# Skip term of tiles 12 to 14 on VectorE, one column of ones for four heads, gate copies and turn-matrix casts on either engine, and a new work list

## The chip, the cores and the metric

One Trainium2 chip; the kernel runs on one of its NeuronCores. A core has TensorE (PE: matmuls, and PEld for its weight loads, which overlap them), VectorE (DVE), ScalarE (ACT), GpSimd (POOL), SyncE (SP, which here only issues transfers) and 16 DMA engines. Each engine runs its instructions in order. Matmuls write to PSUM, eight banks of 512 fp32 columns here; VectorE and ScalarE move results from there to SBUF, which frees the bank. The metric is device microseconds of one execution, the median of several runs.

## The reference, cut to what matters

For x of 2048 rows and 512 columns, a state-space layer and a linear attention with softmax features, mixed by a gate:

```python
g = sigmoid((x * gate_w).sum(-1, keepdims=True))
a = 2 * real(C @ h) + x * Dskip              # h: scan over rows, h = Lam_bar*h + B_bar x
q, k, v = x @ wqkv                           # 32 heads of 16
phi(t) = concat(softmax(t @ w_phi), softmax(-t @ w_phi))
kv = phi(k)^T v ;  z = sum over rows of phi(k)
b = (phi(q) @ kv) / (phi(q) @ z + 1e-6) @ wo
out = g * a + (1 - g) * b
```

## The kernel before

The 2048 rows are 16 tiles of 128. Everything is issued by a list of tokens, `ORDER` (lines 24 to 54), which is walked once: each token resumes a generator that issues the instructions of one small step, so the list sets the order on every engine. A token may carry `@b` (the PSUM bank that the step takes) and `:D` (the step's copy runs on VectorE; without it on ScalarE, through `evac`, line 139, or `scaled`, line 468).

The tokens that matter here:

- `Lk`, `Lx`, `Lv`, `Lb`, `Lq`, `Lc`, `Lo`, `Ld`: loads on SP's queue. `Lx` gives two plain loads of x (tiles 0 and 1) and then seven transposing loads into `xT`, two tiles each (tiles 2 and 3 by the first, 10 and 11 by the fifth; line 244). `Lv` loads the v weights into `WKV` (267), `Lb` the two halves of B into `C2` (249) and transposes them into `BT` (252). `Ld` loads the skip vector, and the rows of x for the tiles in `XD`, into space that `WKV` no longer needs.
- `Z`: small matmuls on zeros that keep TensorE at work at the start. `W`, `T`, `f`: transposes of the k weights and of x's first tiles, and the folding of the feature weights into the k weights.
- `k0` to `k15`: key features of a tile, four matmuls of 480 columns (521), then a cast into `Xq`. `v0` to `v15`: values of a tile, four matmuls of 512 columns (521), then a cast into one of eight buffers `vx`. `q0` to `q15`: query features, 481 columns, of which the last is the gate's logit; after the cast a step writes the clamped, negated logit into `nge` (555).
- `x`, `n`, `e`, `s` with a group of key tiles (`X`, `N`, `E`, `S` of query tiles): maximum, minimum, exponentials and sums of the softmax features. `a`: the sums over keys, 128x128 weights against 68 columns of `vx` (645): four heads of 16 values, and a column of ones behind each head. `Y`: these sums through a mask into `KVm` (845, 847).
- `b`, `g`, `z`, `sa`, `sb`, `H`: the scan over rows: matmuls with `BT` (655, 660), with the turn matrices `dg` (672 to 690, 757 to 773), and additions into `HH` (750). `Da`, `Db`: the turn matrices, three casts into `dgv` each (458, 460) and products (463) on VectorE.
- `hd`, `hk`, `ek`, `dk`: scaled copies (470, 472) and additions that make the remaining rows' states `LS`.
- `y0` to `y15`: the state-space output of a tile: eight 512-column matmuls (876) and, for a tile outside `XD`, the skip term as four 128-column matmuls (883). `o`: attention numerators (893), a reciprocal by way of logarithm and exponential, and a product on VectorE (907). `O`: their transposes by DMA. `t`: four matmuls with `wo` (932) and the scaling by the gate `G` (938 on ScalarE, 940 on VectorE). `u`: for a tile in `XD` the gated skip term on VectorE (912), added in the tile's evacuation (936). `G`: the gate from `nge`. `R`: the stores.

Tile numbers of `y`, `o`, `t` follow the order of the output, not of `x`. `y0` and `o0` come after the sums over keys are complete.

Of the kernel before, what the change touches and what calls it, by code (L numbers as in the profile page):

```python
# [14 lines left out]
BF16 = mybir.dt.bfloat16  # L15
# [10 lines left out]
f1 f0 T0:D Lx f2@4 V@3 T1@2 f3@6 Lx V f2 Z k0@5 P T1:D U P f3 k1@2 k1 Lv P2 P k0 P2 U k3@1 P2 k2@6 P2 k7@4 P2 P4 P3  # L26
P2 P3 P4 U Lx P4 i i M i Lb x0z U k5@0 k4@3 k1 M k3 k0 V2@1 i k7 i v0@4 n0 k5 x0 M k2 Lb v1@6 x0 n0 V2 k6@2 Lx v6@1
k4 i v3@3 k8@5 n0 x0 n0 x1 k9@0 n1 x0 Lx x1 L x0 n1 k10@7 n0 k6 v1 x2 M2 M2 Lx Lb x2 v6 e0 k11@2 x1 n1 x2 Lb k8 n1
x1 x2 x1 Da k13@5 v3 v0 Lq n2 k12@4 k15@3 k14@1 n1 dc n2 e1 s0 k9 k11 n2 x2 n2 b10@0 Da k15 k14 n2 Lc k10 s0 b10 k13
# [20 lines left out]
S3 y11 dk0 S3 dk2:D t8 dk0:D dk0 dk0 dk2 R3 dk0 t9 dk2 O5 dk0 dk4 dk2 t10 dk4:D dk4 dk2 dk4:D y14@6 t8 dk4 t10 t11  # L50
t9 S3 dk6:D o12@4 o13@1 S3 dk6 o12 R4 y13@3 y12@7 o12 dk6:D o13 dk4 o13 o12 o14@4 o13 dk6 o14 R2 o14 dk6 dk6 y15@12
o14 y13 y12 o15@4 u11 y12 o15 y14 t11 o15 y14 y13 O6 t12 O7 R5 t13 t14 o15 O8 t12:D t13:D t14:D y15 R6 R7 y15 t15
t15 R8 t15 t15:D R8
# [27 lines left out]
def kernel(  # L81
# [57 lines left out]
    def evac(out_ap, in_ap):  # L139
        if sel["eng"] == "act":  # L140
            nc.scalar.copy(out=out_ap, in_=in_ap)  # L141
        else:
            nc.vector.tensor_copy(out=out_ap, in_=in_ap)
# [171 lines left out]
    m16 = maskN[:].rearrange("p a b -> p (a b)")  # L315
    order = [2 * g + q for g in ORD for q in range(2)]
    live = {}
    MM = nc.tensor.matmul
# [134 lines left out]
        yield  # L453

    def st_D(k0, k1):
        TT, TC = VT, nc.vector.tensor_copy
        nk = k1 - k0
        TC(out=dgv[0:HS, k0:k1].rearrange("p k m h f -> p k h m f"), in_=dgs[0:HS, k0:k1].unsqueeze(4).to_broadcast([HS, nk, 2, MT, 4]))
        for h in range(2):
            TC(out=dgv[HS:P, k0:k1, :, h, :], in_=dgs[HS:P, k0:k1, 1 - h].unsqueeze(3).to_broadcast([HS, nk, MT, 4]))  # L460
# [81 lines left out]
    def st_v(ti):  # L542
        pv = bank([P, D], F32, "pv")
        tile_mm(pv, KO[ti], Wv)
        yield
        evac(vxb[ti % NVX][:, :, 0:Dh], pv[:].rearrange("p (h e) -> p h e", e=Dh))
        yield

    def st_q(n):
# [4 lines left out]
        yield
        VS(out=nge[:, n:n + 1], in0=pq[:, DF:DF + 1], scalar1=-Z_MAX, scalar2=-1.0, op0=ALU.max, op1=ALU.mult)
# [93 lines left out]

# [369 lines left out]
```

## Time and profile before

| | us |
|---|---|
| median of 3 runs (146.64 to 147.11) | 146.94 |
| the profiled execution's own time | 146.7 |
| its span, first to last instruction of the profile | 144.7 |
| TensorE busy | 138.2 |
| VectorE busy | 132.9 |
| ScalarE busy | 125.4 |
| GpSimd busy | 21.9 |

In the rows below, times are microseconds from the span's start, a row of the chain or timeline gives start, duration and what ran, `x24` is a number of instructions merged into the row, `[0.18 <-DMA ...]` says that the engine stood idle that long before it and what ended the wait. In a row of a group, what follows the bar is total busy time, mean ns of one instruction, and idle time before them. A row of windows gives for each engine the busy time and number of instructions. Matmuls are pipelined and their ends are modelled, so that TensorE's busy time contains short waits; these are found from the starts of successive rows.

### The profile page before, as it was taken

To read this page: it belongs to the slowest core of one execution; us is meant where nothing else is said; L and a number is where in the kernel's file an instruction comes from. 1 tells how busy PE (TensorE), PEld (TensorE's weight loads), DVE (VectorE), ACT (ScalarE), POOL (GpSimd) and SP (SyncE) were. 2 spreads that over 40 slices of the span, in tenths; PEclk is the share of its full clock that TensorE was granted. 3 is DMA by queue.
4 is the path that set the end of the run, shared out by engine and by line. 5 is a ranking of instruction groups with operands and counts; after the bars stand their busy time and mean duration, and the time that the engine had idled before them with its cause. 6 is when DMAs were issued, how large, how long until landed. Compare 5 with 4: busy or idle time off the path is not lost.

```text
span 144.7 us, 2815 instructions
## 1 busy us (share of the span) xinstructions
PE 138.2 (96%) x971; PEld 74.9 (52%) x986; DVE 132.9 (92%) x313; ACT 125.4 (87%) x245; POOL 21.9 (15%) x40
## 2 busy tenths in 40 slices
PE   6999999999999999999999999999999999999990
PEld 4854444444545465544445556656454545455550
DVE  5389999999999999999999999999999999999560
ACT  0899998999999999999999999999999996984110
POOL 7100807900000000190000336000000000000000
PEclk9999999999999999999999999999999999999998
DMA  4999998997030058079929857886896989995441
GB/s 115 219 231 230 202 184 201 174 212 131 5 70 2 0 128 239 0 67 107 181 64 210 211 89 116 146 173 150 202 112 127 273 189 243 210 290 163 117 137 36
DMA packets 55957, 21.56 MB, mean 149 GB/s; under 512 B 44552, under 2 KB 55944, under 8 KB 55944
## 3 DMA queue, kind: packets, MB, share of 16 engines
q1 hardware_dynamic: 52688, 18.98, 63.1%
q0 software_dynamic: 2240, 2.10, 11.1%
q10 hardware_dynamic: 1016, 0.32, 0.9%
q8 instruction: 7, 0.11, 0.4%
q14 instruction: 6, 0.05, 0.1%
HBM read 3.30 MB, written 2.10 MB: 37 GB/s over the span
## 4 chain that ended last, share of the span: by engine, by line
PE 79%; DMA 9%; SPq 4%; DVE 3%; issue 1%; ACT 1%; ACTq 0%
PE PS L521 20%; PE PS L876 17%; PE PS L660 10%; PE PS L655 10%; PE PS L932 9%; DMA xT<-in_A_x_dram 7%; PE PS L645 3%; SPq L244 3%; PE PS L893 2%; DMA CS<-in_B_wqkv_dram 2%; PE PS L672 2%; PE PS L883 2%; DVE HH L750 1%; PE PS L678 1%; SPq L249 1%
## 5 line engine op out<-in xcount | busy, mean ns | idle before, releaser
L594 ACT ACTIVATE EE<-EE 128x2048 bf16<-128x2048 bf16 x16 | 31.8, 2002 | 0.5 <-DVE EE L587 0.5
L521 PE MATMUL PS<-WKV,xT 128*128 128x480 bf16 (+1 forms) x124 | 28.8, 373 | 0.4 <-DMA xT<-in_A_x_dram 0.2
L521 PEld LDWEIGHTS <-xT 128*128 128x128 bf16 x192 | 18.3, 99 | 19.1 <-DMA xT<-in_A_x_dram 0.6
L876 PE MATMUL PS<-C,LS 128*128 128x512 bf16 (+1 forms) x102 | 22.7, 362 | 0.1
L141 ACT CAST Xq<-PS 128x480 bf16<-128x480 f32 x32 | 19.0, 640 | 0.2
L655 PE MATMUL PS<-xT,BT 128*128 128x512 bf16 x64 | 16.1, 379 | 0.0
L141 ACT CAST LS<-PS 128x512 bf16<-128x512 f32 x24 | 15.8, 735 | 0.1
L521 PE MATMUL PS<-Wq,xT 128*128 128x481 bf16 x64 | 15.6, 368 | 0.0
L660 PE MATMUL PS<-xT,BT 128*128 128x512 bf16 x64 | 15.5, 379 | 0.0
L932 PE MATMUL PS<-Wo,oT 128*128 128x512 bf16 (+2 forms) x64 | 14.8, 366 | 0.2
L569 DVE TENSOR_TENSOR EE<-EE 128x256 bf16<-128x256 bf16 (+3 forms) x54 | 14.6, 302 | 0.0
L876 PEld LDWEIGHTS <-LS 128*128 128x128 bf16 x104 | 9.3, 98 | 9.3 <-DVE LS L822 0.3
L938 ACT ACTIVATE ot<-PS,G 128x512 bf16<-128x512 f32 (+1 forms) x11 | 7.0, 671 | 5.4 <-PE PS L932 5.3
L907 DVE TENSOR_TENSOR on<-PS,rd 128x512 bf16<-128x512 f32 x16 | 10.6, 680 | 0.5 <-ACT rd L901 0.4
L470 ACT ACTIVATE CT<-HH,dgs 128x512 bf16<-128x512 bf16 x16 | 11.1, 722 | 0.0
L569 DVE TENSOR_TENSOR EE<-Xq 128x1024 bf16<-128x1024 bf16 (+1 forms) x18 | 11.0, 623 | 0.0
L141 ACT CAST vx<-PS 128x512 bf16<-128x512 f32 x16 | 10.9, 710 | 0.0
L470 ACT ACTIVATE CT<-CS,nsn 128x512 bf16<-128x512 bf16 x15 | 10.6, 726 | 0.0
L580 DVE TENSOR_TENSOR EE<-Xq,EE 128x2048 bf16<-128x2048 bf16 (+1 forms) x9 | 10.0, 1110 | 0.0
L587 DVE TENSOR_TENSOR EE<-EE,Xq 128x2048 bf16<-128x2048 bf16 (+1 forms) x9 | 9.9, 1105 | 0.0
L660 PEld LDWEIGHTS <-BT 128*128 128x128 bf16 x64 | 6.1, 98 | 6.9 <-issue 0.2
L932 PEld LDWEIGHTS <-oT 128*128 128x128 bf16 x68 | 6.2, 98 | 6.6 <-DMA oT<-on 0.7
(175 smaller groups left out, 252.7 us busy)
## 6 DMA issues: line engine op xcount, KB each, us to landing
out_dram<-ot SPq DMA_DIRECT2D x7, 256.0 KB, 2.5
C<-CS SPq DMA_DIRECT2D x4, 256.0 KB, 3.1
C<-CT POOLq DMA_DIRECT2D x4, 256.0 KB, 8.3
CS<-HH SPq DMA_DIRECT2D x8, 128.0 KB, 3.4
LS<-CT POOLq DMA_DIRECT2D x4, 256.0 KB, 3.7
CS<-LS SPq DMA_DIRECT2D x2, 512.0 KB, 6.4
WKV<-in_B_wqkv_dram SPq DMA_DIRECT2D x1, 512.0 KB, 4.7
C<-in_A_B_re_dram SPq DMA_DIRECT2D x1, 512.0 KB, 6.4
```

Of the source, the lines that this page charges most:

```text
L141: nc.scalar.copy(out=out_ap, in_=in_ap)
L470: nc.scalar.mul(out=out_ap, in_=in_ap, mul=s_)
L521: MM(out=pt[:], lhsT=xT[:, kt, ti * P:(ti + 1) * P], rhs=W[:, kt, 0:pt.shape[-1]], start=(kt == 0), stop=(kt == KT - 1))
L569: VT(out=dst, in0=cur[:, :, :, 0:n, :], in1=cur[:, :, :, n:2 * n, :], op=op)
L580: VT(out=half(EE, 0), in0=X5, in1=live["mx", p].to_broadcast([P, L, 8, Dh, 4]), op=ALU.subtract)
L587: VT(out=t, in0=live["mn", p].to_broadcast([P, L, 8, Dh, 4]), in1=X5, op=ALU.subtract)
L594: aexp(out=EE[:, l_:l_ + w], in_=EE[:, l_:l_ + w], func=ACT.Exp)
L655: MM(out=pt[:], lhsT=BT[:, m, kt, :], rhs=cells(kt, r), start=(kt == 0), stop=False, skip_group_check=True)
L660: MM(out=pb[:], lhsT=BT[:, m, kt, :], rhs=cells(kt, 2 * pr), start=(kt == 0), stop=(kt == KT - 1))
L876: MM(out=py[:], lhsT=hs[m], rhs=C2[:, m, c:c + w], start=(m == 0), stop=False)
L907: VT(out=live["on", g_][:, u], in0=pn[:, :, :, 0:Dh], in1=rd[:].unsqueeze(3).to_broadcast([P, 2, 16, Dh]), op=ALU.mult)
L932: MM(out=py[:], lhsT=oT[:, g, :], rhs=Wo[:, g, c:c + w], start=False, stop=(g == HG - 1))
```

## The change

1. `XD`, the tiles whose skip term runs on VectorE, is now 12, 13 and 14, and not 10 and 11.
2. A `vx` buffer holds 65 columns for four heads, 64 values and one column of ones, and not 68; `a` multiplies by 65 columns, and `Y` takes the one sum for all four heads.
3. The step that writes a tile's gate logit into `nge` is a plain copy, on ScalarE unless the token has `:D`; clamp and negation are a first step of `G`, for eight tiles at once.
4. The casts of `Da` and `Db` go through `evac` too, so to ScalarE unless the token has `:D`.
5. `ORDER` is a new list.

```diff
-Lk Z@0 Lk Z Z Z Z B Z B Z Z Z Z Z Lx Lx Z Z Z Z W00@2 Lx W01@1 W00 W01 W00 W01 W10@3 W11@4 W11:D f1@2 f0@1 T0@5 W10
...
+B B Lk Z@0 Z Lk Z Z Z Z Z Z Z Z W01@1 Lx Z W00@2 Z W01 W00 Lx W01 Z Z W00 W11@3 W10@1 T0@2 f1@4 f1 f0@5 W11:D V@3 Lx
...
-XD = (10, 11)
+XD = (12, 13, 14)
...
+    AW = 4 * Dh + 1
...
-    vxb = [pAC.tile([P, H, Dh + 1], BF16, name=f"vx{k}") for k in range(NVX)]
+    vxb = [pAC.tile([P, NB, AW], BF16, name=f"vx{k}") for k in range(NVX)]
...
     def st_D(k0, k1):
-        TT, TC = VT, nc.vector.tensor_copy
+        TT, TC = VT, evac
...
-        evac(vxb[ti % NVX][:, :, 0:Dh], pv[:].rearrange("p (h e) -> p h e", e=Dh))
+        evac(vxb[ti % NVX][:, :, 0:AW - 1], pv[:].rearrange("p (m x) -> p m x", m=NB))
...
-        VS(out=nge[:, n:n + 1], in0=pq[:, DF:DF + 1], scalar1=-Z_MAX, scalar2=-1.0, op0=ALU.max, op1=ALU.mult)
+        evac(nge[:, n:n + 1], pq[:, DF:DF + 1])
...
-                   rhs=vxb[n_ % NVX][:, 4 * m:4 * m + 4, :].rearrange("p h e -> p (h e)"),
+                   rhs=vxb[n_ % NVX][:, m, :],
...
     def st_G(g):
         ns = slice(8 * g, 8 * g + 8)
+        VS(out=nge[:, ns], in0=nge[:, ns], scalar1=-Z_MAX, scalar2=-1.0, op0=ALU.max, op1=ALU.mult)
+        yield
```

What the new list does is seen in the instructions of an engine. First the start of SP's queue; `C_69` takes the two halves of B, `WKV` the v weights. Before:

```order
L235 DMA CS<-in_B_wqkv_dram 128x512 x2
L240 DMA CS<-in_A_x_dram 128x512 x2
L244 DMA_TRANSPOSE xT<-in_A_x_dram 128x4x256 x3
L267 DMA WKV<-in_B_wqkv_dram 128x4x512
L244 DMA_TRANSPOSE xT<-in_A_x_dram 128x4x256
L249 DMA C_69<-in_A_B_re_dram 64x8x512
L249 DMA C_69<-in_A_B_im_dram 64x8x512
L244 DMA_TRANSPOSE xT<-in_A_x_dram 128x4x256 x3
L252 DMA_TRANSPOSE BT<-C_69 128x8x128 x2
```

And now:

```order
L236 DMA CS<-in_B_wqkv_dram 128x512 x2
L241 DMA CS<-in_A_x_dram 128x512 x2
L245 DMA_TRANSPOSE xT<-in_A_x_dram 128x4x256 x2
L268 DMA WKV<-in_B_wqkv_dram 128x4x512
L245 DMA_TRANSPOSE xT<-in_A_x_dram 128x4x256
L250 DMA C_69<-in_A_B_re_dram 64x8x512
L245 DMA_TRANSPOSE xT<-in_A_x_dram 128x4x256
L250 DMA C_69<-in_A_B_im_dram 64x8x512
L245 DMA_TRANSPOSE xT<-in_A_x_dram 128x4x256 x3
```

The v weights stand ahead of the third transpose, and the fourth transpose stands between the halves of B. TensorE, in the same stretch, now runs k0, k1, k2, k3, v3, k4, v0, k7, k5, k6, v6, v1, k11, k9, k10, k8, and ran k0, k1, k3, k2, k7, k5, k4, v0, v1, k6, v6, v3, k8, k9, k10, k11.

Second, the casts on ScalarE that follow these tiles: `Xq` takes a tile of k, `vx_126` to `vx_132` tiles of v (v0 is 126, v1 127, v3 129, v6 132), `EE` is an exponential. Before:

```order
L514 ACT_TABLE_LOAD
L141 CAST Xq<-PS 128x8x60
L141 CAST vx_127<-PS 128x32x16
L141 CAST vx_132<-PS 128x32x16
L594 ACTIVATE EE<-EE 128x2048
L141 CAST Xq<-PS 128x8x60
L141 CAST vx_129<-PS 128x32x16
L141 CAST vx_126<-PS 128x32x16
L451 ACTIVATE decay<-ssm_par 128x512
L594 ACTIVATE EE<-EE 128x2048
L141 CAST Xq<-PS 128x8x60 x5
```

And now:

```order
L142 CAST vx_126<-PS 128x8x64
L142 CAST dgv<-dgs 64x3x2x8x4
L142 CAST dgv<-dgs 64x24x4 x2
L142 CAST vx_132<-PS 128x8x64
L594 ACTIVATE EE<-EE 128x2048
L142 CAST vx_127<-PS 128x8x64
L142 CAST Xq<-PS 128x8x60 x2
L142 CAST dgv<-dgs 64x2x2x8x4
L142 CAST dgv<-dgs 64x16x4 x2
L142 CAST Xq<-PS 128x8x60 x2
L594 ACTIVATE EE<-EE 128x2048
L142 CAST Xq<-PS 128x8x60 x3
```

Six casts for the turn matrices stand among them. The last three rows of `Xq` hold k11 and k8, then k10 and k13, then k9, k15 and k12.

Third, VectorE where the sums over keys are finished: `HH` is an addition of the scan, `KVm` the masked sums, `on` a product of `o`. Before:

```order
L750 TENSOR_TENSOR HH<-PS,HH 128x4x128
L845 TENSOR_TENSOR KVm<-PS,maskN 128x16x16
L847 SCALAR_TENSOR_TENSOR KVm<-PS,eps_p,maskN 128x16
L845 TENSOR_TENSOR KVm<-PS,maskN 128x16x16
L555 TENSOR_SCALAR nge<-PS 128x1
L847 SCALAR_TENSOR_TENSOR KVm<-PS,eps_p,maskN 128x16
L750 TENSOR_TENSOR HH<-PS,HH 128x2x256 x2
L629 TENSOR_TENSOR EE<-EE,rho 128x32x64
L555 TENSOR_SCALAR nge<-PS 128x1 x2
L907 TENSOR_TENSOR on<-PS,rd 128x512 x2
```

And now:

```order
L750 TENSOR_TENSOR HH<-PS,HH 128x4x128
L847 TENSOR_TENSOR KVm<-PS,maskN 128x16x16
L850 SCALAR_TENSOR_TENSOR KVm<-PS,eps_p,maskN 128x16
L847 TENSOR_TENSOR KVm<-PS,maskN 128x16x16
L750 TENSOR_TENSOR HH<-PS,HH 128x2x256
L850 SCALAR_TENSOR_TENSOR KVm<-PS,eps_p,maskN 128x16
L750 TENSOR_TENSOR HH<-PS,HH 128x2x256
L629 TENSOR_TENSOR EE<-EE,rho 128x32x64
L569 TENSOR_TENSOR EE<-Xq 128x32x32
L911 TENSOR_TENSOR on<-PS,rd 128x512 x2
```

The gate copies are gone from here, and one of the two additions into `HH` stands a step earlier.

More of the change, by code (lines that the diff above doesn't have):

```diff
@@ L24 @@
 ORDER = """
-Lk Z@0 Lk Z Z Z Z B Z B Z Z Z Z Z Lx Lx Z Z Z Z W00@2 Lx W01@1 W00 W01 W00 W01 W10@3 W11@4 W11:D f1@2 f0@1 T0@5 W10
[L26 to L29, printed above, removed]
@@ L50 @@
[L50 to L53, printed above, removed]
+B B Lk Z@0 Z Lk Z Z Z Z Z Z Z Z W01@1 Lx Z W00@2 Z W01 W00 Lx W01 Z Z W00 W11@3 W10@1 T0@2 f1@4 f1 f0@5 W11:D V@3 Lx
+W10:D T0:D T1@1 f0 f2@2 V P Z T1:D P f3@3 P2 f2 Lx U f3 P2 Lv P P2 P2 P2 P4 P4 P4 k0@4 k1@1 k1 k1 k0 P3 P3 k2@3 i Lx
@@ new lines @@
+Lb i k0 Lx k2 U n0 U k3@1 k3 Lb Lx x0 v3@4 k4@1 v0@3 P2 i k7@2 x0 Lx i i V2@5 x1 n1 M x0 k5@6 x1 Lx x1 i Z Lb k6@7 M
+v3 n0 M x0 v6@0 n0 U x0z V2 L k5 k6 x1 v1@6 n1 x1 x0 k4 Lb n0 k7 v0 Lc n0 n1 x2 k11@1 n2 Da x2 n1 n2 x2 v6 k9@3 Ld
+n2 M2 k10@0 M2 Lc M2 k8@2 k13@7 e0 n2 v1 k12@6 s0 Lq n1 s0 k15@5 k11 k8 Da b10@2 b11@1 Db k10 x2 b00@0 k13 b20@7 x2
+s0 e1 s0 Db k9 Lc n2 k14@3 k15 k12 s0 g20@6 b00 s1 Lq b31@0 n3 Lb s1 b20 g10@7 b10 g11@2 x3 s0 g20 Da c1:D e2 g00@5
+Da k14 b11 g00 g10 b01@1 x3 b21@3 e2 s1 Lc b30@4 b31 x3 g20 c2 n4 s0 g10 s1 g11 w1@7 g01@6 w2@0 b21 b01 x4 g21@1 Lb
@@ new lines @@
+s1 g11 dc g30@3 s2 b30 n3 w3@4 g30 w2 w1 x4 g00 Db c1:D g21 c2 g30 g21 s2 w0@5 c3 w0 g21 x4 c3:D n3 g31@7 x3 c0:D s2
+g11 g01 g31 g01 C w3 gw g31 c0:D x3 s2 n3 g31 g21 g11 x4 v4@5 g11 g01 s2 s1 n3 g21 n4 c0:D q3@4 v4 g31 g31 g11 g11
+n4 s2 x4 q2@3 g31 g01 q3 g31 C g11 v2@5 s1 e3 g11:D c2:D g31 g21 v2 q0@2 n4 g01:D q3:D g31:D g01 g21:D q1@7 a0@40
+g01 q2 q1 q1 s2 q0 g01 g01 n4 g21 g21 a0 v7@5 q0 b40@7 z0@2 z0 a1 c3:D a1 z0 v5@1 a2 e3 c1:D e4 z0 q2 v5 X0 b50@2 A
+N0 X0 q7@6 q9@3 q10@1 z0 v7 s3 b50 q9 z0@2 q9 q4@5 q6@3 q7 a2 b40 a2 X0 s3 q10 C N0 z0 N0 b61@7 q10 q4 A b70@1 q4
@@ new lines @@
+q5@5 z0 q6 s3 X0 q6 e4 b70 g70@3 z0 sa0@1 a2 N0 b61 X0 s3 N0 s4 q5 v8@7 g70 X1 q7:D N1 g40@2 E0 v11@6 g40 sa0 s4 E0
+q5 X1 q8@1 b71@5 s3 Ld g70 N1 v11 b60@3 g71@6 b71 sb0@5 S0 s4 S0 X1 g71 S0 v8 g50@7 G0 X1 g71 C N1 b60 s3 g50 s4
+v9@3 N1 S0 s4 G0 q8 q8 g40 g71 v10@2 sb0 H1@1 S0 H0@5 A g50 v9 X1 N1 S0 s4 q11@3 g60@7 H1 g60 v10 g61@1 S0 E1 b51@2
+g60 E1 S0 A g61 b51 g51@7 q11 g71 Ld H0 g61 b41@5 G0 XX0 s3 g61 q11 S1 a3 s4 Lo hd1 b41 g51 g41@3 g71 XX0 g51 S0 g41
+S1 g41 a3 hd0 g51 g41 g71 XX0 a3 hd1 a3 g61 g61 S0 g41 g41 g71 g51 G0 q13@5 N2 g61 g51 g51 g71 hd0 XX0 g41 g41 g61
@@ new lines @@
+X2 g51 S1 v13@2 N2 g41 g71 g61 g51 g41 X2 N2 g61 hd0 q12@6 g51 v13 z1@7 q13 hd0 z1 v12@1 X2 hd1 q14@2 z1 hd0 z1 q12
+q13 N2 z1 S1 z1@7 v12 z1 z1 v15@3 X2 S1 hd1 v15 z1 X2 a4 sa1@1 hd1 v14@7 S1 v14 q14 y0@3 a4 sa1 hd0 N2 sb1@7 q12 END
+sb1 XX1 a4 q14 a4 q15@2 Y Y H3@7 XX1 H2@6 S1 E2 q15 Y y0 H3 Y hk6 o2@4 H2 XX1 o3@0 y1@7 o3 y1 y3@6 o2 o3 S1 hd1 o2
+E2 y1 y0 X3 o2 q15 XX1 o3 o0@4 hk4 o0 o0 o1@0 y2@2 X3 o1 o1 y3 S2 hk4 y3 y2 hk4 hk6 y2 o0 S1 o1 hk6 o5@0 hk4 S2 hk4
+S2 o4@4 o4 o5 N3 S2 O1 o4 X3 O0 o4 hk6 o5 t2 hk6 t3 t2 y4@4 hk4 t0 S2 t3 S2 N3 ek0 S1 ek0 S2 t1 t0 o5 hk6 N3 O2 ek0
@@ new lines @@
+G1 y5@0 S2 N3 ek0 ek0 o6@2 o7@5 X3 o6 ek0 o6 t1 ek2 y5 y4 y4 y7@7 ek2 X3 y5 y6@1 ek4 o7 ek2 o7 ek2 y7 o6 y7 N3 t4 R1
+t5 ek4 E3 S2 ek2 t4 o7 o8@5 G1 ek4:D ek2 ek4:D o9@2 o8 ek6:D S2 t5 ek6:D y6 ek6:D ek6:D ek4 ek6 o9 O3 XX2 ek4 o8 ek6
+o8 o9 E3 o9 dk0 XX2 y6 y10@4 S3 y8@0 y10 G1 dk2 y10 o10@5 y8 o11@2 S3 S3 o10 t6 o10 o11 o11 o10 S3 o11 R2 t6 y8 t7
+O4 S3 S3 S3 dk0 dk0:D S3 y11@1 y11 dk0 G1 y9@2 y9 dk0 R0 S3 dk2:D dk2:D y9 y11 t7 t8 O5 dk2:D dk2 dk0 S3 dk4:D t9 S3
+t10 t8 dk4 dk4:D t11 dk4:D t10 dk2 dk4 y14@0 t11 dk6:D o12@3 o12 o13@6 o12 o13 dk6:D dk4 o12 o13 y12@1 R3 y13@5 o13
@@ L54 @@
+o14@3 dk6 dk6 o14 dk6 R5 y15@67 o14 O6 dk6 o14 t9 y14 o15@2 y12 y13 t12 u12 o15 o15 o15 u14 t13 O7 t14 t12 y15 R4
+u13 t13 t14 O8 R6 y15 t15 t15:D t15 R7 t15 R8 R8
 """
@@ L455, in st_D @@
     def st_D(k0, k1):
-        TT, TC = VT, nc.vector.tensor_copy
+        TT, TC = VT, evac
         nk = k1 - k0
-        TC(out=dgv[0:HS, k0:k1].rearrange("p k m h f -> p k h m f"), in_=dgs[0:HS, k0:k1].unsqueeze(4).to_broadcast([HS, nk, 2, MT, 4]))
+        TC(dgv[0:HS, k0:k1].rearrange("p k m h f -> p k h m f"), dgs[0:HS, k0:k1].unsqueeze(4).to_broadcast([HS, nk, 2, MT, 4]))
         for h in range(2):
-            TC(out=dgv[HS:P, k0:k1, :, h, :], in_=dgs[HS:P, k0:k1, 1 - h].unsqueeze(3).to_broadcast([HS, nk, MT, 4]))
+            TC(dgv[HS:P, k0:k1, :, h, :], dgs[HS:P, k0:k1, 1 - h].unsqueeze(3).to_broadcast([HS, nk, MT, 4]))
         yield
@@ L635, in acc @@
     def acc(m):
-        return live["acc"][m // 4][:, m % 4 * KVW:(m % 4 + 1) * KVW]
+        return live["acc"][m // 4][:, m % 4 * AW:(m % 4 + 1) * AW]
     def st_a(n):
@@ L842, in st_Y @@
         for b in range(2):
-            a3 = live["acc"][b][:, 0:4 * KVW].rearrange("p (g h e) -> p (g h) e", h=4, e=Dh + 1)
-            k3 = KVm[:, 4 * b:4 * b + 4, :].rearrange("p g (h e) -> p (g h) e", e=Dh + 1)
-            VT(out=k3[:, :, 0:Dh], in0=a3[:, :, 0:Dh], in1=m16.unsqueeze(2).to_broadcast([P, 16, Dh]), op=ALU.mult)
+            a3 = live["acc"][b][:, 0:4 * AW].rearrange("p (g x) -> p g x", x=AW)
+            k3 = KVm[:, 4 * b:4 * b + 4, :].rearrange("p g (h e) -> p g h e", e=Dh + 1)
+            VT(out=k3[:, :, :, 0:Dh], in0=a3[:, :, 0:AW - 1].rearrange("p g (h e) -> p g h e", e=Dh),
+               in1=maskN[:].unsqueeze(3).to_broadcast([P, 4, 4, Dh]), op=ALU.mult)
             yield
-            nc.vector.scalar_tensor_tensor(out=k3[:, :, Dh], in0=a3[:, :, Dh], scalar=eps_p[:], in1=m16, op0=ALU.add, op1=ALU.mult)
+            nc.vector.scalar_tensor_tensor(out=k3[:, :, :, Dh], in0=a3[:, :, AW - 1:AW].to_broadcast([P, 4, 4]), scalar=eps_p[:], in1=maskN[:],
+                                           op0=ALU.add, op1=ALU.mult)
             yield
```

23 lines of the change are left out of this document (1 added, 22 removed).

## The prediction

> **What bounds the kernel now.** I read the busy shares first, then the slices, then the chain of work that ended last, in order of time.
>
> ```profile
> PE 138.2 (96%) x971; PEld 74.9 (52%) x986; DVE 132.9 (92%) x313; ACT 125.4 (87%) x245; POOL 21.9 (15%) x40
> PE   6999999999999999999999999999999999999990
> PE 79%; DMA 9%; SPq 4%; DVE 3%; issue 1%; ACT 1%; ACTq 0%
> ```
>
> TensorE is busy from end to end and makes 79% of the chain; VectorE and ScalarE are nearly as full. So work taken off VectorE or ScalarE pays only where TensorE waits for them, and a microsecond in which TensorE stands still is lost unless it is won back at another wait. I look for TensorE's waits. After the start the chain leaves it at three places:
>
> ```profile
> 10.89 9.50 DMA xT<-in_A_x_dram
> 20.44 5.04 PE PS L521 x24
> 25.48 0.86 PE PS L660 x4
> ...
> 82.61 0.32 ACT HH L141
> ...
> 90.97 0.73 DVE HH L750
> ...
> 96.15 0.22 PE PS L883 x4
> 96.37 0.51 PE PS L893 x16
> ...
> 140.73 0.58 ACT ot L938
> ```
>
> These are a load of x that ends at 20.4, ScalarE at 82.6 (0.32 us), and VectorE's work at 91 around the sum over keys and values. What TensorE really loses at the last is in its timeline:
>
> ```profile
> 93.09 0.67 PE L893 MATMUL PS<-KVm,phT 128*128 128x68 bf16 x16
> 93.92 1.02 PE L876 MATMUL PS<-C,HH 128*128 128x512 bf16 x4 [0.17 <-DVE HH L750]
> 95.13 1.02 PE L876 MATMUL PS<-C,HH 128*128 128x512 bf16 x4 [0.18 <-DVE nge L555]
> ```
>
> Sixteen 68-column matmuls take 0.51 us and four of 512 columns 0.86 (chain, x16 at 96.37 and x4 at 25.48), so from 93.09 to 93.92 TensorE stands still for 0.32, and from 93.92 to 95.13 for 0.35. With the 0.32 at 82.6 that is 0.99 us; I find no other standstill of that size before the last matmul ends at 140.73. Behind it lie 5.97 us of the profiled run's 146.7.
>
> **The early load.** Here I think the change is decided. The x tiles come as seven transposing loads of two tiles each on SP's queue; its timeline:
>
> ```profile
> 3.29 4.03 SPq L244 DMA_TRANSPOSE xT<-in_A_x_dram  x3
> 7.36 0.58 SPq L267 DMA_DIRECT2D WKV<-in_B_wqkv_dram  x1
> 7.99 1.41 SPq L244 DMA_TRANSPOSE xT<-in_A_x_dram  x1
> 9.44 0.74 SPq L249 DMA_DIRECT2D C<-in_A_B_re_dram  x1
> 10.22 0.63 SPq L249 DMA_DIRECT2D C<-in_A_B_im_dram  x1
> 10.89 9.16 SPq L244 DMA_TRANSPOSE xT<-in_A_x_dram  x3
> ```
>
> The fifth transpose (tiles 10 and 11) is issued at 10.89 and lands 9.50 later, at 20.39. TensorE meets it there:
>
> ```profile
> 8.29 5.87 PE L521 MATMUL PS<-WKV,xT 128*128 128x480 bf16 x28
> 14.20 6.06 PE L521 MATMUL PS<-WKV,xT 128*128 128x512 bf16 x27
> 20.44 5.04 PE L521 MATMUL PS<-WKV,xT 128*128 128x480 bf16 x24 [0.18 <-DMA xT<-in_A_x_dram]
> ```
>
> The old list puts 14 tiles (k0 to k9, v0, v1, v3, v6) ahead of k10, the first user, and they end just as the load lands: 0.18 us lost. The transfer is late because the DMA engines are full, not because it is issued late (windows of 2 us; the last two columns are the DMA share and GB/s):
>
> ```profile
> 4.00:6.00 2.00, 2.00 (x18) 1.88 (x17) 0.54 (x1) 1.39 (x3) 0.03 (x1) 1.00 0.87 199
> 6.00:8.00 2.00, 2.00 (x26) 1.73 (x24) 0.90 (x3) 2.00 (x5) 0.00 (x0) 1.00 1.17 215
> 16.00:18.00 2.00, 2.00 (x11) 0.92 (x10) 2.00 (x7) 1.94 (x4) 1.84 (x6) 1.00 1.21 182
> ```
>
> The new list keeps the same loads ahead of the fifth transpose (four transposes, the v weights, both halves of B) and changes only their order: the weights go ahead of the third transpose, and the fourth goes between the halves of B. The same bytes on full engines land at the same time; only the 0.87 between 4 and 6 leaves room, 0.13 x 2 = 0.26 us. I keep 20.4, bounds 19.9 and 20.6.
>
> But the new list lets TensorE come for tile 11 after 12 tiles, not 14: k11 stands ahead of k8 and k9. A tile of 480 columns takes 0.86 x 480/512 = 0.81 to 5.04/6 = 0.84, and I use 0.82; eight of them and four v tiles of 0.86 are 10.0 us, which from the start at 8.3 ends at 18.3. TensorE then stands for about 2 us, whenever exactly it arrives. The standstill is not itself the price: what is left behind 20.4 is, and that now holds k8 and k9, which used to fill the time. Price: 2 x 0.82 = **+1.64 us** (1.62 to 1.68).
>
> The Trainium skill, *TensorE: Matmul & The Clock Gate*, section "Back-to-back issue gap", gives a sustained roofline of about 131 ns for a 512-column matmul with its weight load. By it the two tiles would cost some 1.0 us (an estimate). The rows here show 0.86 for four, 215 ns each, and the sum goes by them.
>
> **The other parts.** Three tiles instead of two have their skip term on VectorE: four 128-column matmuls fewer, **-0.22** (96.15). The summing matmuls shrink from 68 to 65 columns, 384 columns in all, by 0.86 us per 2048 **-0.16**; nothing if their weight loads set the pace. What moves between VectorE and ScalarE, by groups of instructions:
>
> ```profile
> L555 DVE TENSOR_SCALAR nge<-PS 128x1 f32<-128x1 f32 x16 | 2.2, 145 | 0.0
> L898 ACT ACTIVATE ld<-PS 128x32 f32<-128x32 f32 x16 | 2.8, 190 | 3.9 <-PE PS L893 3.6
> L460 DVE CAST dgv<-dgs 64x96 bf16<-64x96 f32 x2 | 0.4, 246 | 0.0
> L141 ACT CAST V<-PS 128x64 bf16<-128x64 f32 x8 | 1.6, 290 | 0.0
> L141 ACT CAST Xq<-PS 128x480 bf16<-128x480 f32 x32 | 19.0, 640 | 0.2
> L594 ACT ACTIVATE EE<-EE 128x2048 bf16<-128x2048 bf16 x16 | 31.8, 2002 | 0.5 <-DVE EE L587 0.5
> L470 ACT ACTIVATE CT<-HH,dgs 128x512 bf16<-128x512 bf16 x16 | 11.1, 722 | 0.0
> L472 DVE TENSOR_SCALAR CT<-CS,nsn 128x512 bf16<-128x512 bf16 x9 | 2.8, 348 | 0.0
> L938 ACT ACTIVATE ot<-PS,G 128x512 bf16<-128x512 f32 x10 | 6.4, 680 | 0.0
> L940 DVE TENSOR_SCALAR ot<-PS,G 128x512 bf16<-128x512 f32 x3 | 2.3, 750 | 1.3 <-PE PS L932 1.1
> ```
>
> VectorE gives up 16 gate copies (2.2), six casts for the turn matrices (6 x 0.246 = 1.5) and three plain evacuations (2.3), 6.0 us. It takes on one more scale of x and one more fused evacuation (at 0.75 each, as L940), two gate copies and two clamps (4 x 0.15), a net four 512-column scales (1.4) and two double ones (1.4), and some five small copies (about 1.5): 6.4. ScalarE takes 14 gate copies (at 0.19, the nearest row, 2.7; from 0.1 to 0.29 each), six casts (at 0.29, 1.7) and two evacuations (1.4), 5.8, and gives up a net four scales (2.9), two double ones (2.9) and four small casts (1.2), 7.0. Both differences are about 1 us or less, of over 125, and lie behind TensorE's work: nothing by their totals. If that cover goes, it is the third rival.
>
> The skip row's load moves up among the transposes of C and of the q weights, and pushes the latter by two issues, 2.7 us by SP's 4.03 for three; with the standstill TensorE folds them some 4 us later, so that costs nothing. The tail stays: its last 384 columns go to VectorE (0.35 to 0.75, under L940's full width) and not to ScalarE (0.58).
>
> The later waits shrink, since TensorE arrives 1.6 us later against VectorE and ScalarE, and the gate copy of 95.13 is off VectorE. All 0.99 us goes if those engines keep their pace; none if they are delayed as well, and in part they are: ScalarE's order has k8's cast ahead of k10's, and k8 is the fourth tile behind the standstill. I take half, **-0.5**.
>
> Sum, on the profiled run: 146.7 + 1.64 - 0.22 - 0.16 - 0.5 = 147.46. That run lies 0.24 under the median of the runs, by which the same sum gives 147.7; I take the middle, **147.6**.
>
> **The rivals.**
>
> *The load comes in time.* If the v weights, issued 1.35 us sooner, keep the DMA engines fuller and the fifth transpose lands by 18.3, TensorE never waits: 0.18 and 0.38 us are gone, 146.7 - 0.56 = 146.1, 146.3 with half the offset. For it speaks the 0.87; against it the 1.17 and 1.21 behind it and the same bytes ahead. The Trainium skill, *DMA: Bandwidth & Descriptors*, section "Latency and other measured facts", gives transposes an effective 261 GB/s; by it this rival would hold, but the trace moves 182 GB/s at 16 to 18. Chance 0.16.
>
> *The standstill is won back.* All 0.99 us of later waits go: 146.7 + 1.26 - 0.99 = 147.0, with half the offset 147.1: no change that the measurement can tell (I count 0.3%, 0.44 us, as that). For it: each wait is shorter than the shift. Against it: a new list makes new waits. Chance 0.18.
>
> *ScalarE becomes the bound.* Its casts free TensorE's banks in strict order. In the new list k8's cast, three turn-matrix casts, those of k10 and k13 and an exponential stand ahead of k9's, whose bank k14 needs. k8 is done at 20.4 + 4 x 0.82 = 23.7; 0.6 + 0.9 + 1.2 + 2.0 + 0.6 (0.59 a cast by 19.0/32) make 29.0. TensorE comes to k14 at 20.4 + 7 x 0.82 + 4 x 0.86 = 29.6, so ScalarE is 0.6 ahead; if it falls 2 us behind its place, TensorE loses 1.4 and wins nothing back: 146.7 + 1.26 + 1.4 = 149.4. Half of that loss is 148.7, with which the range is made. Chance 0.16.
>
> **How the numbers follow.** The forecast has 0.50, its own range 147.1 to 148.3. Faster (under 146.5): the first rival and a little, 0.17. Within 0.3%: the second and the low part of the forecast, 0.27. Slower (over 147.4): 0.56. The range, 146.3 to 149.0, reaches from the first rival to within the third.
>
> **What would show it.** A wait of TensorE's weight loads for xT of 1.5 to 2.2 us that ends near 20.4 shows the main step right; no wait there shows it wrong. Gate copies on ScalarE should be 0.1 to 0.29 us. The gaps near 82 and 93 us should shrink; if they grow, or one opens near 29 us for ScalarE, the third rival holds. If the last matmul ends before 140.5, I am wrong.

## The result and the profile after

| | before | changed |
|---|---|---|
| median, us | 146.79 (6 runs, 146.45 to 147.73) | 148.93 (5 runs, 148.50 to 149.82) |
| profiled execution, its span | 146.7, 144.7 | 149.82, 147.8 |
| ratio to before, 95% interval | | 1.0143 (1.0095 to 1.0191) |

Medians here and below leave out slow executions, among them one of the changed kernel that took 209.78 us at a granted clock of 0.66, and one of 512.01 us in an experiment.

The change made the kernel 1.4% slower, about 2.1 us by the ratio; I had forecast 147.6. The range, 146.3 to 149.0, holds the median just inside its upper end. The profiled execution of the changed kernel is the slowest of the five, 0.9 us above their median, so its waits are rather too long than too short.

First the page of the changed kernel: busy shares, TensorE's slices and the shares of the chain that ended last.

```profile
PE 137.9 (93%) x967; PEld 74.1 (50%) x982; DVE 133.1 (90%) x304; ACT 124.1 (84%) x257; POOL 22.0 (15%) x40
PE   6998949999999999999999999999999999899990
PE 60%; DMA 15%; DVE 14%; SPq 6%; issue 3%; DVEq 0%
```

TensorE's work is the same within 0.3 us, and VectorE's within 0.2. The span is 3.1 us longer, so what is new is idle time: one slice (18 to 22 us) is half empty, and a late one has a small hole. TensorE's share of the chain fell from 79% to 60%; transfers and VectorE took it. TensorE's timeline gives the places (start, duration, instructions, in brackets the idle time ahead):

```profile
7.66 3.40 PE L521 MATMUL PS<-WKV,xT 128*128 128x480 bf16 x16
11.74 3.56 PE L521 MATMUL PS<-WKV,xT 128*128 128x512 bf16 x15 [0.68 <-ACT Xq L142]
21.17 5.84 PE L521 MATMUL PS<-WKV,xT 128*128 128x480 bf16 x28 [2.20 <-DMA xT<-in_A_x_dram]
90.49 0.41 PE L757 MATMUL PS<-HH,dg 128*128 128x64 bf16 x4 [0.16 <-DVE HH L746]
127.08 0.61 PE L887 MATMUL PS<-Dd,xT 128*128 128x128 bf16 x8
128.23 1.90 PE L936 MATMUL PS<-Wo,oT 128*128 128x512 bf16 x8 [0.54 <-DMA oT<-on]
130.41 1.90 PE L936 MATMUL PS<-Wo,oT 128*128 128x512 bf16 x8 [0.28 <-DMA oT<-on]
```

Three kinds of wait are new: v3 waits 0.68 for the bank that k0's cast frees; k11 waits 2.20 for the fifth transpose of x; and near the end `t` waits twice for a transpose of `on`. Of the old waits at 82 and 93 us, 0.99 in all, mainly the one at 90.49 is left, 0.32 by the starts. The chain in order of time tells why the last ones are late:

```profile
11.87 9.25 DMA xT<-in_A_x_dram
21.17 5.84 PE PS L521 x28
...
99.30 0.27 PE PS L897 x8
99.61 0.61 DVE Xq L569
...
108.26 1.14 DVE EE L629
109.45 5.09 DMA phT<-EE
...
124.03 0.60 DVE on L911
124.65 5.71 DMA oT<-on
130.41 1.90 PE PS L936 x8
...
143.78 0.62 DVE ot L944
```

From 99 us until the transfer of 124.65 lands it runs through VectorE and the transposes of VectorE's results, not through TensorE. The last matmul ends at 143.78; it was 140.73, so 3.05 us later. VectorE fell behind early, which the windows of 10 us show (busy time of PE, PEld, DVE, ACT, POOL, each with its count, then granted clock, DMA share, GB/s). Before:

```profile
10.00:20.00 10.00, 9.95 (x49) 4.55 (x48) 9.76 (x41) 9.56 (x17) 3.25 (x8) 1.00 1.18 211
20.00:30.00 10.00, 9.82 (x48) 4.51 (x47) 9.91 (x24) 9.49 (x15) 6.16 (x10) 1.00 0.96 201
30.00:40.00 10.00, 9.95 (x59) 4.96 (x58) 10.00 (x25) 9.99 (x20) 0.00 (x0) 1.00 0.57 103
```

After:

```profile
10.00:20.00 10.00, 8.24 (x39) 3.51 (x37) 8.96 (x36) 8.97 (x19) 3.32 (x3) 1.00 1.38 194
20.00:30.00 10.00, 8.83 (x43) 4.22 (x44) 9.14 (x20) 8.70 (x15) 5.86 (x15) 1.00 0.91 159
30.00:40.00 10.00, 9.95 (x51) 4.65 (x50) 8.95 (x19) 10.00 (x18) 0.00 (x0) 1.00 0.84 157
```

Between 10 and 40 us TensorE did 2.70 us less than before and VectorE 2.62 less (29.67 against 27.05). In the first 10 us VectorE had done 0.6 more than before (6.27 against 5.68) and TensorE 0.1 less, so that at 40 us VectorE is 2.0 behind and TensorE 2.8. Both are nearly full from there to 120 us. What VectorE waits for in this stretch is ScalarE:

```profile
11.79 0.42 DVE L569 TENSOR_TENSOR EE<-Xq 128x512 bf16<-128x512 bf16 x1 [0.87 <-ACT Xq L142]
22.50 0.69 DVE L569 TENSOR_TENSOR smk<-EE 128x1024 bf16<-128x1024 bf16 x1 [0.41 <-ACT EE L594]
28.78 0.69 DVE L569 TENSOR_TENSOR smk<-EE 128x1024 bf16<-128x1024 bf16 x1 [0.34 <-ACT EE L594]
34.26 0.69 DVE L569 TENSOR_TENSOR EE<-Xq 128x1024 bf16<-128x1024 bf16 x1 [1.05 <-ACT Xq L142]
```

These four are 2.67 us; the kernel before has no such row between 8 and 45 us. The first experiment shows which of them belong to the load.

### The profile page after: what moved, and what is told of

Read it like the earlier page. It is cut to its first block, busy times and chain, and to the rows that moved or that the text cites. A ratio compares the mean times of both kernels' runs of the same rounds, so it can differ in the third digit from the quotient of the medians.

```text
span 147.8 us, 2808 instructions
## 1 busy us (share of the span) xinstructions
PE 137.9 (93%) x967; PEld 74.1 (50%) x982; DVE 133.1 (90%) x304; ACT 124.1 (84%) x257; POOL 22.0 (15%) x40
## 4 chain that ended last, share of the span: by engine, by line
PE 60%; DMA 15%; DVE 14%; SPq 6%; issue 3%; DVEq 0%
PE PS L521 19%; PE PS L655 10%; PE PS L660 9%; PE PS L880 8%; DMA xT<-in_A_x_dram 6%; SPq L245 4%; DMA oT<-on 4%; PE PS L936 3%; DMA phT<-EE 3%; DVE on L911 3%; PE PS L645 3%; DVE Xq L569 2%; PE PS L672 2%; DVE LS L822 2%; DMA Wc<-in_B_w_phi_dram 2%
## 5 line engine op out<-in xcount | busy, mean ns | idle before, releaser
L594 ACT ACTIVATE EE<-EE 128x2048 bf16<-128x2048 bf16 x16 | 30.7, 1944 | 0.3 <-DVE EE L587 0.2
L142 ACT CAST Xq<-PS 128x480 bf16<-128x480 f32 x32 | 17.3, 579 | 2.1 <-PE PS L521 2.0
L942 ACT ACTIVATE ot<-PS,G 128x512 bf16<-128x512 f32 (+1 forms) x13 | 8.5, 652 | 9.5 <-PE PS L936 9.5
L142 ACT CAST LS<-PS 128x512 bf16<-128x512 f32 x24 | 14.3, 634 | 0.3 <-PE PS L660 0.3
L470 ACT ACTIVATE CT<-CS,nsn 128x512 bf16<-128x512 bf16 x17 | 11.9, 723 | 0.0
L142 ACT CAST vx<-PS 128x512 bf16<-128x512 f32 x16 | 9.8, 631 | 0.0
L470 ACT ACTIVATE CT<-HH,dgs 128x512 bf16<-128x512 bf16 x13 | 9.5, 729 | 0.0
```

The source lines that it names most:

```text
L470: nc.scalar.mul(out=out_ap, in_=in_ap, mul=s_)
L594: aexp(out=EE[:, l_:l_ + w], in_=EE[:, l_:l_ + w], func=ACT.Exp)
```

## The experiments

Each ratio is to the kernel before on the same chip, since that kernel's own median moved between 146.8 and 147.6 from one set of runs to the next. The theory after the result: TensorE stands early for the fifth transpose, VectorE falls behind as well, and because both are full the loss comes out at the end. The rivals: the order of the loads made the transpose late; the edits of code cost by themselves; what happens early is without effect, since the list's later order sets the end.

**k8 in the place of k11.** The two names change places in the list; banks and everything else stay.

```diff
-k11@1 n2 Da x2 n1 n2 x2 v6 k9@3 Ld n2 M2 k10@0 M2 Lc M2 k8@2 k13@7 e0 n2 v1 k12@6 s0 Lq n1 s0 k15@5 k11 k8 Da
+k8@1 n2 Da x2 n1 n2 x2 v6 k9@3 Ld n2 M2 k10@0 M2 Lc M2 k11@2 k13@7 e0 n2 v1 k12@6 s0 Lq n1 s0 k15@5 k8 k11 Da
```

> The new list with the places of k8 and k11 exchanged, loads untouched: only k10 of the first fourteen tiles still needs the fifth transpose, and it comes behind k8 and k9. Load theory (what is lost is the work that stands behind the fifth transpose, and VectorE and ScalarE being late afterwards follows from it): TensorE's wait for xT falls from 2.2 us to 0.3 to 1.2, since the two tiles fill 1.64 us; the last matmul ends 1.6 to 2.7 us sooner, a time of 146.4 to 147.5 beside 149.1. Rival (the list's later order on VectorE, or the new work on ScalarE, sets the end whatever happens early): the wait falls as much, but the waits for oT and phT behind 117 us grow by as much, and the time stays at 148.6 or above.

Measured: 148.75 us, ratio 1.0081 (1.0051 to 1.0111). TensorE's timeline:

```profile
17.07 8.53 PE L521 MATMUL PS<-WKV,xT 128*128 128x480 bf16 x40
38.11 0.37 PE L477 MATMUL PS<-BD,phT 128*128 128x120 bf16 x4 [0.48 <-ACT LS L142]
129.50 1.90 PE L936 MATMUL PS<-Wo,oT 128*128 128x512 bf16 x8 [0.71 <-DMA oT<-on]
```

Ten tiles of k run without a gap: the wait for xT is gone. But the gain is 0.6%, some 0.9 us, well under the 1.6 to 2.7 of the load theory. A wait for ScalarE opens at 38, and the late wait for oT stays. VectorE's busy time between 10 and 40 us comes back from 27.05 to 28.25, not to 29.67: its waits at 28.78 and 34.26 are gone, and the first two of the four stay (0.86 and 0.40). So the load is a real part of the loss and of VectorE's lag, and not the whole of either.

**The loads in the old order.** On SP's queue the third transpose goes ahead of the v weights again, and the fourth ahead of both halves of B.

```diff
-Lx U f3 P2 Lv
+Lx U f3 P2 Lx
...
-k2@3 i Lx
-Lb i k0 Lx
+k2@3 i Lv
+Lx i k0 Lb
```

> The new list with the loads of x, of the v weights and of B on SyncE's queue in the order of the old one (third transpose ahead of the v weights, fourth ahead of both halves of B), tiles untouched. Load-order theory (the changed order makes the fifth transpose land at 21.1 and not at 20.4): it lands at 20.2 to 20.6, TensorE's wait for xT falls to about 1.5 us, time 148.2 to 148.6; the v weights land about 1 us later and may cost v3 up to 0.4 us of that. Rival (the landing is set by the bytes on full engines, or by chance): it lands at 20.9 or later, time 148.9 to 149.3.

Measured: 149.34 us, 1.0153 (1.0086 to 1.0220), no better than the changed kernel. The transpose was issued at 11.39 and landed at 20.93; v3 now waited 1.18 us for the v weights. The rival holds: the order of these loads is not why the load was late. With k8 and k11 exchanged too:

> Both edits, k8 and k11 exchanged and the loads in the old order. Load theory: the wait for xT is under 0.6 us and the time 146.0 to 147.0, at or below the kernel before. Rival (late order or new work sets the end): 148 or above.

Measured: 148.95 us, 1.0100 (1.0064 to 1.0136), the same as the exchange alone. The load theory's 146 to 147 was wrong.

How late the transpose lands goes by the execution, in either list. Chains of five other profiles (issue, time to landing), in this order: the old list with the other edits and the old list relieved of work (both below) have the old order of loads; the changed kernel with copies on VectorE and the changed kernel relieved (below) have the new one; the last is the experiment above.

```profile
11.59 11.03 DMA xT<-in_A_x_dram
```

```profile
11.37 9.83 DMA xT<-in_A_x_dram
```

```profile
12.07 8.28 DMA xT<-in_A_x_dram
```

```profile
12.25 8.34 DMA xT<-in_A_x_dram
```

```profile
11.39 9.54 DMA xT<-in_A_x_dram
```

It lands at 22.62, 21.20, 20.35, 20.59 and 20.93, beside 20.39 before and 21.12 after: a spread of 2.3 us, and the old order of loads has both the second earliest and the latest. Not all of these kernels are alike in this stretch; the two pairs that are, which differ only in what was left out behind 100 us, lie 0.8 apart (20.39 and 21.20) and 0.5 (21.12 and 20.59).

**The edits of code in the old list.** `ORDER` and `XD` are those before (one more `G0` and `G1` for the clamps); the layout of the ones, the gate copies and the casts for the turn matrices are those of the change.

```diff
-XD = (12, 13, 14)
+XD = (10, 11)
```

> The old list and the old two tiles with the skip term on VectorE, with the other edits of code: the 65-column layout of the ones, gate copies raw on ScalarE with one clamp for eight tiles, casts for the turn matrices on ScalarE. If the edits of code cost nothing (my prediction: -0.16 at most from the narrower matmuls, 0 where weight loads set the pace): 146.5 to 147.0, level with before, and the whole loss is the list's. If ScalarE, which takes 16 gate copies at 0.2 us and six casts at 0.27, 4.8 us in all, is close behind TensorE in the old list: 147.5 to 149.

Measured: 150.36 us, 1.0184 (1.0127 to 1.0241): slower than the changed kernel. What TensorE waited for in this run:

```profile
PE PS L521 <- DMA xT<-in_A_x_dram: 2.9, 1, 2.9
PE PS L655 <- ACT nge L142: 0.6, 2, 0.3
PE PS L521 <- ACT nge L142: 0.2, 1, 0.2
```

Three waits for a gate copy on ScalarE, 0.8 us in all, which the kernel before and the changed one do not have, and from 27.7 to 71 us the chain that ended last is ScalarE's. The load is 2.9 in this profile, by its late landing. To separate the edits, the same kernel with copies and casts on VectorE again:

```diff
-Da
+Da:D
...
-q3
+q3:D
```

This shows the cast step of `Da` and the copy step of `q3`; `Db` and the other fifteen `q` likewise.

> The old list with the 65-column layout of the ones and one clamp for eight tiles, but the gate copies and the casts for the turn matrices on VectorE as in the kernel before; the skip tiles stay 10 and 11. If the narrower matmuls are worth what my sum had for them, -0.16 us: ratio 0.998 to 1.000; if their weight loads set the pace: 1.000 to 1.002 (two clamps of 0.17 us more on VectorE). Either shows that the old list's 1.018 with the other edits came from moving copies and casts to ScalarE in an order not made for it. Rival (the layout of the ones costs, or the late landing of the load in that profile was the whole of it): 1.006 or more.

Measured: 147.70 us, 1.0006 (0.9972 to 1.0041). The layout of the ones and the clamp cost nothing and bring nothing that the measurement can tell; the sums over keys by form, before and here:

```profile
L645 PE MATMUL PS<-vx,EE 128*128 128x68 bf16 x128 | 5.9, 194 | 0.0
```

```profile
L645 PE MATMUL PS<-vx,EE 128*128 128x65 bf16 x128 | 6.0, 194 | 0.0
```

65 columns take what 68 took. The 1.8% of the experiment before was the move of 22 small instructions to ScalarE, in a list not made for it.

**The copies back on VectorE in the new list.** The same `:D` edits, in the changed kernel.

> The new list with the gate copies of all sixteen q tiles and the six casts for the turn matrices back on VectorE (14 and 6 instructions change the engine), nothing else. If moving them to ScalarE costs by itself: faster than the changed kernel, a ratio to before of 1.010 or less beside its 1.014. If it is right for the new list, because VectorE is the engine that is behind there (20 x 0.15 to 0.25 us, about 3.6 us more work on it): the late waits for oT and phT grow and the ratio is 1.020 to 1.035.

Measured: 155.13 us, 1.0547 (1.0475 to 1.0619), far beyond even the upper bound, and 4.0% beyond the changed kernel's 1.0143. The row of TensorE's timeline with its longest wait, and VectorE's row from the list of waits:

```profile
54.72 0.27 PE L724 MATMUL PS<-V,Sw 128*128 128x256 bf16 x1 [2.08 <-DVE nge L144]
```

```profile
DVE nge L144 <- ACT Xq L142: 5.0, 4, 2.0
```

Twenty copies of 0.15 to 0.25 us are 3 to 3.6 us of work, but four of them made VectorE stand 5.0 us for a cast of ScalarE into `Xq`, the step ahead of the copy in `q`, with all its other work behind them. In the changed kernel most gate copies stand behind that cast in ScalarE's own queue. Not all of the loss is such waiting, for about a microsecond after TensorE's wait of 2.08 the granted clock falls:

```profile
50.00:60.00 10.00, 7.92 (x67) 4.07 (x65) 8.40 (x15) 7.05 (x11) 3.79 (x4) 0.83 0.26 26
```

It is 0.50 from 56 to 59 us, where four matmuls of 512 columns take 1.69 us and not 0.86; in the changed kernel it is 1.00 throughout. That is about 1.7 us of the 8 (0.17 of these 10 us). All four executions show a mean clock of 0.985 to 0.989, so they all have it or something like it; what lowered the clock, no run here shows. The rest is still some 2.8% beyond the changed kernel (an estimate: 4.0% less 1.7 of 147 us). So the move is right for this list: list and edit belong together, and neither can be costed by itself.

**Is VectorE's lag a loss of its own?** The two subtractions for the last four q tiles are left out, in the changed kernel and in the kernel before.

```diff
-        VT(out=half(EE, 0), in0=X5, in1=live["mx", p].to_broadcast([P, L, 8, Dh, 4]), op=ALU.subtract)
+        if p != "G3":
+            VT(out=half(EE, 0), in0=X5, in1=live["mx", p].to_broadcast([P, L, 8, Dh, 4]), op=ALU.subtract)
...
-        VT(out=t, in0=live["mn", p].to_broadcast([P, L, 8, Dh, 4]), in1=X5, op=ALU.subtract)
+        if p != "G3":
+            VT(out=t, in0=live["mn", p].to_broadcast([P, L, 8, Dh, 4]), in1=X5, op=ALU.subtract)
```

> The changed kernel without the two subtractions of the maximum and the minimum for the last four q tiles on VectorE (1.22 us each, at about 111 and 113 us); this part of the computation is left out. VectorE theory: VectorE is late from 99 us on and sets the end through the loads of oT, so the time falls by 0.8 to 1.5 us, to a ratio of 1.004 to 1.009 beside 1.014, with no wait for oT above 0.2 us. Rival (TensorE alone sets the end): within 0.3 us of the changed kernel, 1.012 to 1.016.

> The kernel before without the same two subtractions (at 107.5 and 108.7 us there). VectorE theory: TensorE waits for nothing of VectorE behind 96 us in this kernel, so the relief gains less than 0.3 us: ratio 0.997 to 1.001. If VectorE set the end here too: 0.993 or less. The early part is that of the kernel before, so its trace also shows where the fifth transpose lands on another execution: at 20.0 to 20.7 if the landing belongs to the kernel, later than 21 if it goes by the run.

Measured: the changed kernel without them 148.51 us, 1.0076 (1.0035 to 1.0117); the kernel before without them 146.83, 0.9992 (0.9950 to 1.0034). The same 2.4 us of VectorE's work is worth nothing that can be told from zero before, and some 0.7%, 1.0 us, after. The chain of the relieved kernel ends as before, but the two waits for oT, 0.54 and 0.28, have become one of 0.34:

```profile
117.81 0.68 DVE LS L824
118.49 1.20 DVE on L913 x2
...
123.57 5.45 DMA oT<-on
129.07 1.90 PE PS L938 x8
```

Only part of the 2.4 us comes through, since ScalarE's work is next in line: the chain runs on ScalarE from 96 to 117 us there. The intervals of the changed kernel and of this one overlap, so the size is uncertain; the next experiment gives a second figure.

**Both together.** k8 for k11, and the two subtractions left out.

> The exchange of k8 and k11 together with the relief of VectorE (the two subtractions for the last four q tiles left out): the ratios were 1.008 and 1.008 apart, 1.014 without either. If the early load and the late VectorE are two losses that add up: 1.000 to 1.004 (what is left is TensorE's own waits, 0.68 us for k0's bank and 0.48 for ScalarE at 38 us, less the 0.5 of the kernel before). If they are one loss seen twice (VectorE late because TensorE stood early): 1.006 to 1.009, no better than either.

Measured: 147.94 us, 1.0049 (1.0022 to 1.0077). Beside the exchange alone (1.0081 (1.0051 to 1.0111)) the relief brings 0.3%, 0.5 us, and the intervals overlap again. Both gains together are 0.94%, of 1.29% if they added up in full. That lies between the two forecasts and nearer to two losses than to one, with an overlap. What is left is 0.7 us, near v3's wait of 0.68 in the other profiles; that this wait is what is left is argued, not shown.

**That wait.** k0's cast goes ahead of the table load on ScalarE, on top of the exchange of k8 and k11.

```diff
-k1 k0 P3 P3 k2@3 i Lx Lb i k0 Lx
+k1 k0 k0 P3 P3 k2@3 i Lx Lb i Lx
```

> The exchange of k8 and k11 and one more edit: k0's cast on ScalarE goes ahead of the table load for the sine, where it stood behind. In the exchange alone v3 waits 0.68 us at 12.5 for the bank that this cast frees, and VectorE 0.86 at 12.6 for the tile. VectorE theory (each microsecond in which VectorE idles before about 124 us comes out at the end, for it is as full as TensorE): both waits go, the time falls by 0.5 to 0.9 us, a ratio to before of 1.002 to 1.005 beside the exchange's 1.008. Rival (what is gained early is lost again at 38 us, where ScalarE was the last): the wait there grows from 0.48 to about 1, ratio 1.006 to 1.010.

Measured: 148.87 us, 1.0095 (1.0063 to 1.0128): nothing gained. TensorE's timeline:

```profile
9.80 2.24 PE L521 MATMUL PS<-WKV,xT 128*128 128x480 bf16 x10
12.78 2.64 PE L521 MATMUL PS<-WKV,xT 128*128 128x480 bf16 x12 [0.74 <-ACT Xq L142]
37.42 0.37 PE L477 MATMUL PS<-BD,phT 128*128 128x120 bf16 x4 [0.47 <-ACT LS L142]
```

The wait is still there, 0.74 in place of 0.68, for another cast, and that at 37 us stays too. VectorE's own wait of 0.86 for k0's cast is down to 0.16, but the one of 0.40 for an exponential has grown to 0.84. So both forecasts failed: neither wait of TensorE went, as the one had it, nor did the one near 38 us grow, as the other had it. The waits moved along ScalarE's queue, which suggests that v3's wait is not one cast's place but ScalarE's pace in this stretch, with a table load among the casts. What would remove it was not found.

**The load sooner.** Instead of tiles, the load is moved: the fifth transpose goes ahead of the second half of B on SP's queue, first in the changed kernel, then in the kernel before.

```diff
-Lb Lx x0 v3@4
+Lx Lb x0 v3@4
```

> The changed kernel with one pair of loads on SyncE's queue exchanged: the fifth transpose of x goes ahead of the second half of B, so that 512 KB less lie before it; tiles and list untouched. At about 200 GB/s that is 2.6 us: it lands at 18 to 19.3 and TensorE's wait for xT is 0 to 0.5 us. Load theory: the time falls by 0.8 to 1.6 us, ratio 1.003 to 1.009 beside 1.014. Rival (the wait moves to B's transposes or the sixth load, or VectorE sets the end whatever TensorE does early): 1.012 or more.

Measured: 148.70 us, 1.0086 (1.0048 to 1.0123), as the exchange of tiles. No wait for xT; v3's 0.68, 0.48 at 38 and 0.72 at 129 for oT remain. Two different repairs of the early load give the same 0.6%, at the slow end of what the load theory had here. Each interval still touches the changed kernel's, 1.0095 to 1.0191; what makes the gain credible is that the four kernels without this wait, and otherwise with all of the change, lie at 1.0081 to 1.0100, and the two with it at 1.0143 and 1.0153.

In the kernel before the two tokens lie further apart:

```diff
-Lb v1@6 x0 n0 V2 k6@2 Lx
+Lx v1@6 x0 n0 V2 k6@2 Lb
```

> The kernel before with the same exchange of the fifth transpose and the second half of B. Its wait for that load went by the execution: 0.18 us in the first profile, 1.33 and 2.92 in two later ones with the same loads. Load theory: no wait for xT, a ratio of 0.990 to 0.998, faster than both kernels. Rival (the wait is covered, or B's first transposes are late in its place at 25 us): 0.998 to 1.003.

Measured: 146.44 beside 147.12 us, ratio 0.9933 (0.9906 to 0.9961), faster than both kernels, and all eight runs lie within 146.10 and 146.87. SyncE's and TensorE's timelines:

```profile
10.24 1.55 SPq L244 DMA_TRANSPOSE xT<-in_A_x_dram  x1
11.84 0.61 SPq L249 DMA_DIRECT2D C<-in_A_B_im_dram  x1
12.49 6.30 SPq L244 DMA_TRANSPOSE xT<-in_A_x_dram  x2
```

```profile
13.63 7.68 PE L521 MATMUL PS<-WKV,xT 128*128 128x512 bf16 x36
21.65 3.41 PE L521 MATMUL PS<-WKV,xT 128*128 128x480 bf16 x16 [0.34 <-DMA xT<-in_A_x_dram]
```

TensorE runs through to 21.3, and a short wait is left for the sixth transpose.

## Why the prediction was right in direction and short in size

- **Bound, early load: right.** TensorE came for k11 after twelve tiles and stood until the fifth transpose landed. The four kernels in which a repair takes the wait away win 0.4 to 0.6%; with that fell the rivals of a load in time and of a standstill won back.
- **"Whenever exactly it arrives" and 20.4 with bounds 19.9 and 20.6: too early and too narrow.** The changed order of these loads is indeed without effect that the runs can tell, but the landing goes by the execution, 20.35 to 22.62, and 20.39 was nearly the earliest of the seven. I had taken the bounds from one profile. The Trainium skill (*DMA: Bandwidth & Descriptors*, "Latency and other measured facts") gives transposes an effective 261 GB/s. The rival that leaned on it, a landing by 18.3, is contradicted by all seven landings; here transposes shared the engines with plain loads, at 159 to 211 GB/s in the windows between 10 and 30 us, and no run shows transposes alone.
- **Price 1.64: about right as a total, but in two waits.** I had TensorE arrive at 18.3; it came at 19.0 in the first profile (21.17 less 2.20) and at 19.6 and 19.7 in those of the relieved kernel and of the copies on VectorE, among other things because v3 is now the fifth tile and waits 0.68 for k0's bank. That wait, which I did not look for, and the one for the load that is left (0.7 to 1.1 us in the other profiles with this list of tiles, 2.20 in the first) make 1.4 to 1.8. The part that the load's repair wins back is 0.9.
- **Later waits "shrink by half, -0.5": right for the waits that it names; the sum had none for new ones.** From the landing on, 0.73 later than before, the last matmul is 3.05 later: 0.73 + 1.64 - 0.22 leaves 0.90 of *more* waiting, where I had 0.5 less. Yet the old waits of 0.99 are down to about 0.4, as my reason had it. What the sum put at nothing is that TensorE would stand for `on`: the eight matmuls at 127.08 take 0.45 (chain, x8), so it stands 0.70 before 128.23, and 0.45 before 130.41, since eight of 512 columns take 1.73. These 1.15 us, with small gaps, make the difference. My reason was that TensorE would come later while VectorE and ScalarE kept their pace; the windows show VectorE losing as much as TensorE in the same 30 us, and the chain shows it setting the end. The relief, worth 0.5 to 1.0 us here and nothing that can be told before, agrees. By the medians 1.3 us is missing in all (148.93 - 147.6), of which 0.16 is the next point.
- **Narrower matmuls -0.16: nothing,** the other end that I had named: 194 ns in the rows either way.
- **Small instructions moved between the engines at no cost: right for the list they came with,** wrong as a rule: 1.8% with the old list, 4.0% if undone in the new one, a part of that at a lower clock. Totals of work said nothing about it. The gate copies took 0.21 us on ScalarE, within the forecast, and 0.33 in the old list.
- **ScalarE as the bound near 29 us: not there,** for TensorE. Its pace does show at v3, in VectorE's early waits, and at 38 us once the load's wait is gone.
- **The skip tile's -0.22** was not tried alone.

What is left open: the last 0.5% after load and VectorE are relieved, near v3's wait in size, where the one attempt failed; and how much of VectorE's lag at the end is the load's, since its early waits for k0's cast and an exponential, 1.3 of 2.67 us, stay without it.

## What to carry to other kernels

Where three engines are all 84% full or more, price an early standstill on each of them: an engine that falls behind with the bottleneck can become the next one. Here TensorE's old waits did shrink, but VectorE's lag opened larger ones near the end, so a sum over known waits must leave room for new ones. Do not cost a small instruction's move by its duration; ask what its queue holds behind it and whose bank it frees. And take a load's slack from several executions, not one profile: here moving 512 KB behind one transpose was worth 0.7% in a kernel whose profile showed a wait of 0.18 us.

## What the runs showed of the hardware

The same transpose behind the same bytes landed between 20.4 and 22.6 us. A 65-column matmul costs as much as one of 68 behind a 128-column weight load (194 ns mean in both groups; sixteen in a row take 0.52 and 0.51 us in the chains). A copy of one column took 0.15 us on VectorE, and on ScalarE 0.21 in the new list and 0.33 in the old one. In the changed kernel with the copies on VectorE the granted clock was 0.50 for over 3 us, from about a microsecond after TensorE had stood 2.08; in the changed kernel, whose wait at 21 us was 2.20, it stayed at 1.00.
